# A Fourier mixing layer and a routed feed-forward layer: the third batch's stage 2 in another order beside blocks 1 to 3

## The chip, the cores and the metric

The kernel runs on one core of one Trainium2 chip. Its time is in microseconds (us) of device time for one launch. A core has TensorE (PE in the profile) with its weight loads (PEld), VectorE (DVE), ScalarE (ACT), GpSimd (POOL) and SyncE (SP), which here only issues DMAs. SP and ACT each have a DMA queue of their own; GpSimd issues the indirect DMAs.

## The reference: what is computed

The first half mixes along the sequence, for 8 batches of 2496 positions and 256 channels; the second sends every one of the 19968 tokens through one of 8 experts, chosen by a hash of its id:

```python
X = np.fft.rfft(x, axis=1)
Y = X * (filt_r + 1j * filt_i)[None, :, :]
y = np.fft.irfft(Y, n=x.shape[1], axis=1)
...
expert_idx = token_ids * np.int64(2654435761) % np.int64(E)
for e in range(E):
    xe = x[expert_idx == e]
    out[expert_idx == e] = np.maximum(xe @ w1[e], 0.0) @ w2[e]
```

Everything is float32. w1 is 8 x 256 x 1024, w2 is 8 x 1024 x 256.

## The kernel before, in words

**The Fourier half** splits 2496 into 39 x 64 and takes each batch through three stages, each cut into pieces.

- *Stage 1* (`stage1`, 6 pieces): `load1` brings x (three loads of three DMAs each, L252, on SP's queue); TensorE multiplies by the small table `wf_t` (tiles `pa`, L264 and L270); ACT copies the result to `mid` (L267, L272); a DMA writes it to a scratch tensor d1 in DRAM (L300 on ACT's queue).
- *Stage 2* (`forward` and `back`, 10 pieces each): `load2` brings d1 back in another layout (5 loads, L306, on SP's queue). `forward(u)` multiplies two slices by the table `d_t` (tile `pb_u`, L315). VectorE then multiplies by the filter: L321 makes y from pb and the filter, the two L325 make z, and L326 adds z to y. `back(u)`, the "way back", multiplies y by the table `e_t` (tile `pc_u`, L338); ACT copies it out (L341), and after every second piece ACT issues two DMAs that write it to the scratch tensor d2 (L345).
- *Stage 3* (`stage3`, 6 pieces): `load4` reads d2 (L409, SP's queue, three loads); TensorE multiplies by `wi_t` (tiles `pd`, L264 and L270); ACT copies to `o`; GpSimd scatters the rows to their place among the experts' tokens (L436).

The tiles pa, pb, pc and pd share four PSUM buffers (`fps`); y and z share three SBUF buffers (`ppool`), which are handed out again in the order of the program.

**The expert half** works in tiles of 256 tokens of one expert. A *block* is one such tile, `step(i)`. In the blocks before the 43rd it goes: GpSimd makes four sums of w1 for the tile after (`weight_sums`, tiles `tw`, L881); TensorE makes the up product (`up`, L891, 7 half-size products, after Strassen), while ACT (L895, L902) and VectorE (L898) put its parts together; then SP is given the load of w1 for the tile after next (L467), VectorE transposes the next tile's tokens (L859) and makes its four token sums (tile `st`, L872); then TensorE makes the down product (`down`, tile `dps`, L926) in four quarters of four matmuls; VectorE copies it out (`osb`, L931), and SP is given the load of w2 (L470). GpSimd writes a block's rows to the output (L1019) one block later. The w1 and w2 loads are skipped when the tile two before had the same expert. `load` (L848, ACT's queue, five DMAs) brings the tokens of a later tile.

**The order of the work** around the change is written by hand. Each engine's instructions stand in the order in which the program issues them. All pieces of the Fourier half that go beside the blocks stand in a list `todo` as (due time, piece). A due time of 2.86 means block 2, share .86. `step(i)` calls `run_until` at four points: in front of the down product (due before i + .6), after its first three quarters (before i + .7, .8 and .9), and behind the w2 load (before i + 1). All pieces that are due are issued there. `spaced` makes evenly spaced due times, and `within` moves them into the second half of their block, so that few stand between the up product's parts. `part1`, `part2` and `part3` make such lists for the three stages; `part2` gives the way back of piece u the due time of the forward piece plus a lag.

The first blocks go like this. Before block 0 the program has done batches 0 and 1, stage 1 of batch 2 ("third") and four pieces of stage 1 of batch 3 ("fourth"). Beside blocks 1 to 3 stand stage 2 of the third batch and the last two pieces of the fourth's stage 1; beside blocks 4 to 7 the third's stage 3; from block 6 the fourth's stage 2. Tiles of the second group of blocks may be loaded only when the third batch's rows are scattered.

A DMA of SP or ACT also waits until the DMA that used the same one of eight semaphores before it, counted over both queues in the order of the program, has landed.

## Time and profile before

| what | value |
|---|---|
| median of 6 runs | 1412.92 us (1409.94 to 1416.84) |
| profiled execution, its own time | 1411.95 us |
| its span | 1410.2 us, 26945 instructions |
| busy: PE, PEld, DVE, ACT, POOL | 97%, 90%, 64%, 30%, 59% |
| DMA | 284.67 MB, mean 202 GB/s |
| mean granted TensorE clock | 0.995 of full speed |

How to read it. The profile is of one execution; its span runs from the first to the last instruction, and the time has 1.75 us more around it. A *timeline* line gives the start from the span's start, the time to the end of the merged group, engine, line of the kernel, operation, tile written <- tiles read, shapes, and the number of merged records; in brackets the idle time of that engine ahead of it and what ended it. Each float32 matmul leaves two records, so "x8" is four matmuls, and their modelled ends overlap the next one's start: the distance of two starts is the better measure. A *waits* line reads: engine, tile and line that waited, <- who ended it, total us, times, longest. "<- issue" means that the profile shows no releaser. A *windows* line gives for each stretch its length, the busy time of PE, PEld, DVE, ACT and POOL with the number of instructions, the granted clock (1.00 is full speed), the DMA engines' share, and GB/s.

Blocks in the time of the span: block 0's up product starts at 140.03 us, block 1's at 156.45, block 2's at 181.67, block 3's at 204.17, block 4's at 224.44 and block 5's at 242.02.

### The profile page before, as it was taken

Reading aid. Unit: us, or ns where it says so; the run is one execution under the profiler, and the core shown is the slowest. Engines: PE = TensorE matmul, PEld = TensorE weight load, DVE = VectorE, ACT = ScalarE, POOL = GpSimd, SP = SyncE. Lnnn points to the kernel's source line nnn. Section 1 sums busy time; section 2 is a strip of 40 time slices with the busy share of each in tenths; the row PEclk is TensorE's granted clock in tenths of the full one; section 3 lists DMA queues with packets and bytes.
Section 4 is the critical chain, followed back from the end, with each engine's and each line's share of the span. In section 5 each row is a group of like instructions: output and inputs, shape, how many; then the busy total and the mean of one; then the engine's idle time right before and its main releaser. Section 6 shows DMA issues by size and latency. Waiting matters only on the chain.

```text
span 1410.2 us, 26945 instructions
## 1 busy us (share of the span) xinstructions
PE 1366.0 (97%) x9618; PEld 1273.1 (90%) x9618; DVE 905.6 (64%) x1708; ACT 421.0 (30%) x776; POOL 832.2 (59%) x736
## 2 busy tenths in 40 slices
PE   8898899999999999999999999999999999999997
PEld 7777888989888988899999988899999999999997
DVE  7773675575556566446665687467767677676775
ACT  4554122223232223232223222223222222222222
POOL 6167243844665565578664678787655556655563
PEclk9999899999999999999999999999999999999999
DMA  8777854857987698798896785867643525161611
GB/s 217 216 237 220 239 192 122 274 188 243 264 279 226 186 303 271 252 298 282 285 275 211 220 248 160 234 214 259 198 132 88 174 73 191 45 222 40 215 47 35
DMA packets 253949, 284.67 MB, mean 202 GB/s; under 512 B 125651, under 2 KB 222342, under 8 KB 243620
## 3 DMA queue, kind: packets, MB, share of 16 engines
q1 hardware_dynamic: 104589, 185.62, 41.2%
q10 hardware_dynamic: 129303, 52.69, 15.5%
q0 software_dynamic: 19920, 44.59, 9.1%
q8 instruction: 79, 1.29, 0.4%
q14 instruction: 58, 0.48, 0.1%
HBM read 302.04 MB, written 86.15 MB: 275 GB/s over the span
## 4 chain that ended last, share of the span: by engine, by line
PE 80%; DMA 9%; DVE 5%; issue 3%; POOL 1%; ACT 1%; ACTq 1%; SPq 0%; POOLq 0%; DVEq 0%
PE dps L926 16%; PE up_b L891 7%; PE dnc L953 5%; PE dnb L953 5%; PE dna L953 5%; PE upa L948 5%; PE upc L948 5%; PE up_a L891 4%; PE up_c L891 4%; PE pd L270 4%; PE pb L315 4%; PE pa L270 3%; PE pc L338 3%; PE upe L948 2%; PE upg L948 2%
## 5 line engine op out<-in xcount | busy, mean ns | idle before, releaser
L926 PE MATMUL dps<-wts,ht 128*128 128x256 f32 x1344 | 310.8, 380 | 1.2 <-ACT ht L895 1.2
L1019 POOL DMA_INDIRECT out_dram<-osb,no x158 | 167.9, 1063 | 224.2 <-DVE osb L960 164.3
L926 PEld LDWEIGHTS dps<-wts,ht 128*128 128x128 f32 x1344 | 253.6, 190 | 38.6 <-issue 1.6
L436 POOL DMA_INDIRECT xs<-o,sidx x176 | 176.6, 1003 | 172.5 <-ACT o L272 65.3
L881 POOL TENSOR_TENSOR tw<-wts 128x512 f32<-128x512 f32 x158 | 204.8, 1296 | 88.6 <-DMA wts<-in_moe_w_dram 42.2
L881 POOL TENSOR_TENSOR tw<-wts,tw 128x512 f32<-128x512 f32 x158 | 205.7, 1302 | 6.2
L898 DVE TENSOR_TENSOR ht<-up_b,ht 128x512 f32<-128x512 f32 x126 | 87.1, 691 | 99.1 <-PE up_b L891 75.9
L325 DVE TENSOR_TENSOR z<-pb,filt 64x512 f32<-64x512 f32 x160 | 110.1, 688 | 31.0 <-PE pc L338 29.0
L895 ACT ACTIVATE ht<-ht 128x512 f32<-128x512 f32 x126 | 79.3, 630 | 154.5 <-DVE ht L898 141.1
L957 ACT ACTIVATE ht<-ht 128x512 f32<-128x512 f32 x114 | 71.9, 631 | 155.9 <-DVE ht L960 107.6
L931 DVE COPY osb<-dps 128x512 f32<-128x512 f32 x42 | 29.1, 692 | 121.8 <-PE dps L926 121.4
L891 PE MATMUL up_a<-xt,wts 128*128 128x128 f32 x672 | 97.4, 278 | 5.1 <-DVE xt L859 3.8
L891 PEld LDWEIGHTS up_a<-xt,wts 128*128 128x128 f32 x672 | 89.3, 194 | 8.0 <-issue 4.0
L891 PE MATMUL up_b<-st,tw 128*128 128x128 f32 x672 | 90.6, 278 | 2.9 <-DVE ht L898 1.8
L891 PEld LDWEIGHTS up_b<-st,tw 128*128 128x128 f32 x672 | 82.5, 193 | 5.0 <-issue 4.7
L341 ACT COPY mid<-pc 128x512 f32<-128x512 f32 x60 | 35.0, 583 | 155.9 <-PE pc L338 86.4
L270 PE MATMUL pd<-t,wi_t 120*117 120x256 f32 x320 | 76.5, 380 | 4.4 <-DMA t<-d 2.7
L953 PE MATMUL dna<-wts,ht 128*128 128x128 f32 x608 | 80.3, 275 | 0.0
L898 DVE TENSOR_TENSOR ht<-up_c,ht 128x512 f32<-128x512 f32 x84 | 58.0, 690 | 31.9 <-PE up_c L891 28.2
L948 PE MATMUL upa<-filt,wts 128*128 128x128 f32 x592 | 78.2, 275 | 0.0
L272 ACT COPY o<-pd 117x512 f32<-117x512 f32 x80 | 45.2, 586 | 100.9 <-PE pd L270 42.2
L199 DVE TENSOR_TENSOR filt<-ht 128x512 f32<-128x512 f32 x76 | 57.4, 755 | 26.4 <-ACT ht L957 26.4
(209 smaller groups left out, 2646.5 us busy)
## 6 DMA issues: line engine op xcount, KB each, us to landing
wts<-in_moe_w_dram SPq DMA_DIRECT2D x162, 1024.0 KB
xg<-xs ACTq DMA_DIRECT2D x321, 64.0 KB
d_t<-t2s SPq DMA_DIRECT2D x19, 1024.0 KB
e_t<-t2s SPq DMA_DIRECT2D x19, 1024.0 KB
mid<-d SPq DMA_DIRECT2D x70, 256.0 KB
d<-mid ACTq DMA_DIRECT2D x60, 256.0 KB
x<-in_x_dram SPq DMA_DIRECT2D x39, 312.0 KB
t<-d SPq DMA_DIRECT2D x12, 960.0 KB
```

What stands on the lines that cost most here:

```text
L270: nc.tensor.matmul(out=ps[0:cols * H, k, :], lhsT=w[:], rhs=src[:, 2 * i + k, :], start=True, stop=True)
L325: nc.vector.tensor_tensor(out=z[b], in0=ps[a], in1=f_t[1][64 * hi:64 * hi + 64, s1:s1 + 2, :], op=OP.mult)
L436: st = nc.gpsimd.indirect_dma_start(out=xs[:], out_offset=bass.IndirectOffsetOnAxis(ap=index, axis=0), in_=rows, in_offset=None, bounds_ch ...
L881: eng.tensor_tensor(t[k][:], p, q, op=OP.subtract)
L891: nc.tensor.matmul(out=ps[bank][:, f, :], lhsT=w[:, f * P:(f + 1) * P], rhs=xx, start=first and f == 0, stop=True, skip_group_check=True)
L895: nc.scalar.activation(out=out, in_=in_, func=AF.Relu)
L898: nc.vector.tensor_tensor(out, ps[bank][:], other, op=OP.add)
L926: nc.tensor.matmul(out=ps[:, h, :], lhsT=ht[:, h, fp, :], rhs=w2[:, fp, :], start=(fp == 0), stop=(fp == FP - 1))
L948: nc.tensor.matmul(out=ps[:, f, :], lhsT=w[:, f * P:(f + 1) * P], rhs=xx, start=first and f == 0, stop=True, skip_group_check=True)
L953: nc.tensor.matmul(out=ps[:, 0, :], lhsT=a[:, f, :], rhs=b[:, f, :], start=first and f == 0, stop=True, skip_group_check=True)
L957: nc.scalar.activation(out=out, in_=in_, func=AF.Relu)
L1019: st = nc.gpsimd.indirect_dma_start(out=out[:], out_offset=bass.IndirectOffsetOnAxis(ap=to_rows[i][:, h:h + 1], axis=0), in_=o[:, h, :], i ...
```

## The change

Three lines of the list are replaced by four. The lists of piece times of stage 2 of the third batch are now written out one by one, without `within`.

```diff
-    todo += part2(2, spaced(1, 3.5, N_2), [None] * 4 + [1.5], .6)
-    todo += part3(2, spaced(4.6, 7.5, NU), [4.0, 4.1, 4.8]) + part1(3, [None] * 4 + [1.5, 2], [None, None, .5])
+    todo += [(t, lambda u=u: third.forward(u)) for u, t in enumerate((1.55, 1.65, 1.76, 1.86, 2.56, 2.65, 2.76, 2.86, 3.56, 3.65))]
+    todo += [(t, lambda u=u: third.back(u)) for u, t in enumerate((1.75, 1.85, 1.95, 2.55, 2.75, 2.85, 2.95, 3.55, 3.75, 3.85))]
+    todo += [(1.77, lambda: third.load2(4))]
+    todo += part3(2, spaced(4.6, 7.5, NU), [3.95, 4.1, 4.8]) + part1(3, [None] * 4 + [3.9, 4.2], [None, None, 1.9])
     todo += part2(3, spaced(6.4, 10, N_2), [5.2, 5.4, 5.6, 6.5, 7.5], .6)
```

No instruction is added or removed. In words, in the order in which TensorE takes them:

| | before | after |
|---|---|---|
| block 1, behind up | pb 0, pb 1, dps, pb 2, dps, pb 3, pa 4, dps, pc 0, dps, pc 1 | pb 0, dps, pb 1, dps, pc 0, pb 2, dps, pc 1, pb 3, dps, pc 2 |
| block 2, behind up | pb 4, pa 5, pc 2, pb 5, dps, pb 6, pc 3, dps, pb 7, pc 4, dps, dps, pc 5 | pc 3, pb 4, dps, pb 5, dps, pc 4, pb 6, dps, pc 5, pb 7, dps, pc 6 |
| block 3, behind up | pb 8, pc 6, pb 9, dps, pc 7, dps, pc 8, dps, dps, pc 9 | pc 7, pb 8, dps, pb 9, dps, pc 8, dps, pc 9, dps, pa 4 |
| block 4, behind up | dps, dps, dps, pd 0, dps | dps, pa 5, dps, dps, pd 0, dps |

(dps is a quarter of the down product; pa 4 and pd 0 are pairs of two tiles; pa is the fourth batch's, all else the third's.) VectorE and ACT follow in the same order. On SP's queue the third x load of the fourth batch moves from between the loads of w1 and w2 of tile 2 to behind w2 of tile 3; the first t load (L409, of d2) moves from behind w1 of tile 6 to in front of it, behind w2 of tile 5; the second stays behind w1 of tile 6. ACT's two DMAs that write the fourth batch's last stage 1 pieces to d1 (L300) move from block 2 to block 4.

## The prediction

> **What bounds the kernel now.** I read the page first (busy shares, chain), then PE's waits between the end of block 1's up product (162.70 us of the span) and the end of block 4 (242.02), then the PE, VectorE and GpSimd timelines of that stretch.

> ```profile
> PE 1366.0 (97%) x9618; PEld 1273.1 (90%) x9618; DVE 905.6 (64%) x1708; ACT 421.0 (30%) x776; POOL 832.2 (59%) x736
> PE 80%; DMA 9%; DVE 5%; issue 3%; POOL 1%; ACT 1%; ACTq 1%; SPq 0%; POOLq 0%; DVEq 0%
> ```

> TensorE is busy 97% of the span and is most of the chain that ended last: nothing in this change removes a matmul, so all it can win is PE's idle time, and all it can lose is new idle time. PE's waits from 157 to 242 us:

> ```profile
> PE pa L270 <- issue: 3.3, 1, 3.3
> PE pd L270 <- DMA t<-d: 1.6, 1, 1.6
> PE up_b L891 <- DVE ht L898: 1.4, 2, 0.9
> PE pc L338 <- DVE y L326: 1.0, 1, 1.0
> ```

> The largest stands in block 1 (PE timeline):

> ```profile
> 167.02 1.89 PE L926 MATMUL dps<-wts,ht 128*128 128x256 f32 x8
> 168.74 1.03 PE L315 MATMUL pb<-mid,d_t 128*128 128x256 f32 x4
> 173.07 3.59 PE L270 MATMUL pa<-x,wf_t 117*120 117x256 f32 x8 [3.30 <-issue]
> 176.49 1.89 PE L926 MATMUL dps<-wts,ht 128*128 128x256 f32 x8
> ```

> The pa pair is the fourth batch's stage 1 piece 4. It needs x, whose three loads SP issues from 163.27 to 169.76. Then it runs 3.42 us where a pair takes 1.73, because of the clock:

> ```profile
> 135.40:138.82 3.42, 0.79 (x8) 0.60 (x6) 0.00 (x0) 0.00 (x0) 2.64 (x3) 1.00 0.52 93
> 138.82:145.65 6.83, 5.62 (x26) 5.65 (x27) 3.60 (x7) 0.59 (x1) 2.34 (x2) 0.50 0.85 194
> 169.54:172.96 3.42, 0.23 (x2) 0.00 (x0) 3.31 (x6) 0.00 (x0) 1.22 (x2) 1.00 0.60 202
> 172.96:176.37 3.41, 3.30 (x8) 2.61 (x9) 2.02 (x3) 0.59 (x1) 0.00 (x0) 0.50 0.84 311
> ```

> After a 3.4 us stretch with PE busy 0.23 or 0.79 us, the granted clock is 0.50 in the next one or two.

> **What PE loses now.** Start-to-start on the timeline: pb or pc 0.865 us, pa or pd pair 1.73, the short pa 1.08, a quarter of dps 1.73, a whole up product 6.25 (156.45 to 162.70). From 162.70 to 242.02 PE does 10 pb and 10 pc (17.3), pa 1.73 + 1.08, pd 1.73, 16 quarters of dps (27.7), 3 up (18.75): 68.3. The stretch is 79.3, so **11.0 us are lost**: block 1 5.1 (3.4 wait, 1.7 half clock); up of block 2 1.25 and of block 3 0.73 (L898 late, VectorE backlog); block 3 1.2 (pc waits for y); up of block 4 0.83 (ACT late after pc's copies); block 4 1.86 (pd waits for t).

> **The change, part by part.** The same instructions are issued, in another order; only waits move.

> *Stage 1 pieces 4 and 5 and their x load go later.* The 3.4 us wait for x and its 1.7 us go: the load is issued behind block 3's w2 load, the piece stands at the end of block 3, some 25 us later. On SP the next weight loads move up: tile 3's w1 is issued at about 167 instead of 172.15. Piece 5's ACT writes of d1 move to block 4; the fourth batch reads d1 in block 5 at the earliest, more than 10 us behind. I take nothing for these two; the cover is that slack.

> *The new order in block 1.* PE's order becomes pb_0, dps, pb_1, dps, pc_0, pb_2, dps, pc_1, pb_3, dps, pc_2. From 162.70, pc_0 is due at 162.70 + 0.87 + 1.73 + 0.87 + 1.73 = 167.9. It needs y_0, and y_0 is VectorE's (timeline of VectorE, then of GpSimd):

> ```profile
> 164.24 0.60 DVE L872 TENSOR_TENSOR st<-xt 128x128 f32<-128x128 f32 x1
> 164.88 1.31 DVE L872 TENSOR_TENSOR st<-st,xt 128x128 f32<-128x128 f32 x1
> 166.11 1.35 DVE L872 TENSOR_TENSOR st<-xt 128x128 f32<-128x128 f32 x1
> 167.38 1.35 DVE L872 TENSOR_TENSOR st<-xt,st 128x128 f32<-128x128 f32 x1
> 168.66 0.68 DVE L321 TENSOR_TENSOR y<-pb,filt 128x512 f32<-128x512 f32 x1
> 169.35 1.39 DVE L325 TENSOR_TENSOR z<-pb,filt 64x512 f32<-64x512 f32 x2
> 170.78 0.69 DVE L326 TENSOR_TENSOR y<-y,z 128x512 f32<-128x512 f32 x1
> ```
> ```profile
> 163.41 1.28 POOL L881 TENSOR_TENSOR tw<-wts 128x512 f32<-128x512 f32 x1 [22.25 <-PE up_b L891]
> ...
> 167.27 1.32 POOL L881 TENSOR_TENSOR tw<-wts,tw 128x512 f32<-128x512 f32 x1
> ```

> The token sums L872 take 1.3 us each beside GpSimd's tw, and 0.29 us in block 2 where it is idle. Nothing before this point is moved, so y_0 ends at 171.47 again. Now pb_2, pb_3 and pa stand between; in the changed order pc_0 stands there at once, and **PE waits from 167.9 to 171.55, 3.65 us**. What is late next is y_0, not x. Behind pc_0 in PE's queue stand all of block 1's rest and the next up.

> *Half clock after that wait.* The trace does not show this wait: the price lies between 0 (the gap of 2.07 us before 47.59 left the clock at 1.0) and 3.4 (half of the 6.83 us at 138.82). The halved stretches keep a beat of their own (138.82 and 172.96 lie 34.14 = 10 x 3.414 us apart), so one of them will hold between 1.8 and 3.4 us of the 3.65; nearest is the stretch at 169.54, so 1.7, which I give 6 in 10.

> [...]

> *Rest of block 1 and up of block 2.* y_1 ends by about 175.3 (its last add is beside tile 3's tw, which now starts near 172; such adds took 0.95 to 1.74 against 0.69); pc_1 is due 175.0 at full clock, after 176 at half: 0 to 0.4. VectorE no longer holds z for pc (now "z L325 <- PE pc L338", 4.2 us at 179.28), so the osb copy and L898 are in time: the 1.25 and 0.73 go, for about 0.

> *Block 2.* Counted from the up's end, y_4 is ready at +6.35 (before: 189.17 and 195.52, with an add of 1.74 beside tw); pc_4 is due at +6.07; pc_5 about the same. 0 to 0.9, I take 0.5.

> *Block 3.* First y at +7.9 from the up's end, since tw is again beside the sums (before: 211.15 and 219.04). pc_8 is due after pc_7, pb_8, dps, pb_9, dps: 6.06. It waits 1.9, then pc_9 0.3: 2.2 instead of 1.2.

> *Block 4.* pc_9 ends 1.0 to 3.5 us sooner against block 4's up, ACT's copy is free: the 0.83 goes. The t load is issued when d2 has landed, at the latest 5.9 us after its issue on ACT (225.25 to 231.17 today): 1.4 to 4 us into block 4's up. It took 7.3 us to pd (231.17 to 238.47). pd is due at 6.25 + 1.73 + 1.08 + 3.46 = 12.5. The 1.86 goes. SP stands still till d2 has landed; behind it is the next w1 load, not due before +5.6.

> **Sum.** New losses: 3.65 + 1.7 + 0 + 0.5 + 2.2 = 8.05, and 0.3 for restarts behind waits (first matmul 0.45 to 0.47 instead of 0.38): **8.35 against 11.0, a gain of 2.7**; without the half clock (and 0.2 at pc_1) 6.85, a gain of 4.2. The profiled execution took 1411.95 (span 1410.2): 1409.25 or 1407.8. It lies 0.97 under the median of the six runs, 1412.92, from which the same gains give 1410.2 and 1408.7. Both versions roll the same dice with the clock, so I put the forecast between: **1409.6**. Behind 242 us PE runs without idle time to 320, so the gain reaches the end.

> [...]

> **Rivals.**
> 1. *y_0 is on time.* If the token sums ran at 0.29 us as in block 2, y_0 would end 6.35 - 1.05 = 5.3 us after the up, due is 5.19: the 3.65 + 1.7 go too, gain 8.0: 1404.9. For it: block 2 does just that. Against: tw of tile 2 waits for nothing that the change moves. Chance 0.18, 1403 to 1407.
> 2. *The change moves waits and wins nothing.* The half clock holds two stretches (+1.7, as at 138.82), block 2 costs 0.9: 10.5 against 11.0, 1412.4. Chance 0.14, 1411.6 to 1414. That the t load does not come sooner belongs here: if it still missed pd by 1.86, gain 0.8.
> 3. *Slower: the t load.* pd_0 has 12.5 us, the load is issued at 1.4 to 4 and took 7.3. If d2's writes and this load together take over 3.9 us more than that, pd waits; over 6.6 more and the kernel is slower than before. At twice 7.3 for the load and 4 for the issue, pd waits 6.1: 2.7 - 6.1, 1416.3. Against: fewer loads are beside it than now. Chance 0.08, 1414 to 1418.

> The forecast's own case has 0.60, 1407.5 to 1411.6. A measurement tells 0.3%, 4.24 us, from no change. Faster than 1408.7: rival 1 (0.18) and half of the forecast without the half clock, which lies on that bound (0.12): 0.30. Slower than 1417.2: the worse part of rival 3 and what I do not see, 0.08. Same: 0.62. The range leaves out the far end of rival 1 and rival 3: 1405 to 1413.5.

> **What would show it.** PE idle about 3.6 us in front of the first pc (L338), released by VectorE's y L326, in place of pa <- issue; granted clock 0.50 for 3.4 us behind it, or not; no wait of up_b for L898 in blocks 2 and 3; about 1.9 us in front of pc_8; no pd <- t; the end of block 4 at 238 to 239.5 instead of 242.02. If pc_0 doesn't wait, rival 1 holds and I misread VectorE's queue; if pd waits, rival 3.

## The result and the profile after

The changed kernel takes 1408.87 us, median of 26 runs (1403.76 to 1412.57), beside 1413.6 for the kernel before (52 runs). The medians differ by 4.7 us. The ratio is 0.9963, with a 95% interval of 0.9952 to 0.9974: 5.2 us faster, 3.7 to 6.8. The prediction was 1409.6, a gain of 3.3 over the 1412.92 of the first six runs. The profiled execution has a span of 1405.8 us (before: 1410.2). Its page, the busy shares:

```profile
PE 1367.3 (97%) x9618; PEld 1274.4 (91%) x9618; DVE 911.8 (65%) x1708; ACT 419.8 (30%) x776; POOL 833.7 (59%) x736
```

Busy shares say nothing here: PE is at 97% in both. PE's waits from 157 to 242 us do. The four lines that the prediction shows, and a fifth of 0.2 us, have become one:

```profile
PE pc L338 <- DVE y L326: 5.7, 2, 3.9
```

pa no longer waits, nor pd, nor up_b for VectorE. The PE timeline shows where the two waits stand (the first pc of block 1, pc_0, and pc_8 of block 3) and that pa and pd have no bracket:

```profile
172.25 1.13 PE L338 MATMUL pc<-y,e_t 128*128 128x256 f32 x4 [3.88 <-DVE y L326]
...
216.14 1.10 PE L338 MATMUL pc<-y,e_t 128*128 128x256 f32 x4 [1.80 <-DVE y L326]
...
221.66 1.89 PE L270 MATMUL pa<-x,wf_t 117*120 117x256 f32 x8
...
236.01 1.89 PE L270 MATMUL pd<-t,wi_t 120*117 120x256 f32 x8
```

The half clock came too. In the windows (length, busy time of PE, PEld, DVE, ACT and POOL, granted clock, DMA share, GB/s) PE is busy 1.03 of 3.41 us, and the next stretch has 0.50:

```profile
169.87:173.28 3.41, 1.03 (x5) 0.93 (x6) 3.30 (x6) 0.00 (x0) 1.61 (x2) 1.00 0.93 315
173.28:176.69 3.41, 3.41 (x10) 2.70 (x9) 3.32 (x5) 0.59 (x1) 2.62 (x2) 0.50 0.46 180
```

y_0 is late for the reason that the prediction gives. VectorE's token sums (L872 before, L874 now) last 1.00 to 1.35 us beside GpSimd's tw, and y_0 ends at 172.19, 9.17 us behind the up product; SP gave out the w1 load that tw needs at 163.86 in this execution. VectorE, then GpSimd, then SP:

```profile
164.57 1.00 DVE L874 TENSOR_TENSOR st<-xt 128x128 f32<-128x128 f32 x1
165.60 1.32 DVE L874 TENSOR_TENSOR st<-st,xt 128x128 f32<-128x128 f32 x1
...
171.50 0.69 DVE L326 TENSOR_TENSOR y<-y,z 128x512 f32<-128x512 f32 x1
```
```profile
164.15 1.27 POOL L883 TENSOR_TENSOR tw<-wts 128x512 f32<-128x512 f32 x1 [22.59 <-PE pb L315]
```
```profile
163.86 0.11 SPq L467 DMA_DIRECT2D wts<-in_moe_w_dram  x1
```

tw starts 0.19 us behind the end of that issue, while tile 3's tw starts 5.5 us behind the issue of its load (168.53 to 173.99). So tile 2's load seems to be one of those that are skipped, and tw waits for SP to come to it and not for its bytes.

All profiles side by side, from the starts of the up products on PE's timeline. The columns 1 to 2, 2 to 4 and 4 to 5 are the distances between the up products of blocks 1 to 2, 2 to 4 and 4 to 5; without waits they would be 19.23, 39.32 and 16.0 in the new order, 74.55 in all (68.3 of the prediction and the up product of block 1).

| profile | 1 to 2 | 2 to 4 | 4 to 5 | 1 to 5 | half clock from | 10 to 25 |
|---|---|---|---|---|---|---|
| before | 25.22 | 42.76 | 17.59 | 85.58 | 172.96 | 286.59 |
| before_again | 24.72 | 43.41 | 17.70 | 85.83 | 172.35 | 286.04 |
| before_3 | 23.41 | 42.81 | 17.63 | 83.85 | none | 286.31 |
| after | 25.04 | 41.58 | 16.08 | 82.70 | 173.28 | 284.70 |
| after_2 | 24.46 | 41.60 | 16.08 | 82.13 | 175.38 | 283.37 |
| after_3 | 23.35 | 41.60 | 16.08 | 81.03 | 172.99 | 286.80 |
| e1_stage1_later | 19.46 | 46.78 | 17.40 | 83.65 | 184.79 | 285.57 |
| e2_order_alone | 23.94 | 41.03 | 16.94 | 81.92 | none | 284.69 |
| e3_w1_sooner | 19.48 | 41.59 | 16.08 | 77.14 | none | 284.86 |
| e4_dummy | 22.33 | 41.60 | 16.08 | 80.00 | none | 285.89 |
| e5_fill_block3 | 19.48 | 39.86 | 16.08 | 75.42 | none | 285.21 |
| e6_old_order_w1 | 18.34 | 43.05 | 18.15 | 79.53 | none | 285.48 |
| e7_best | 19.48 | 39.87 | 16.08 | 75.42 | none | 286.44 |

### The profile page after: what moved, and what is told of

Same layout as the page of the kernel before. It is cut to its first block, busy times and chain, and to the rows that moved or that the text cites. A ratio compares the mean times of both kernels' runs of the same rounds, so it can differ in the third digit from the quotient of the medians.

```text
span 1405.8 us, 26942 instructions
## 1 busy us (share of the span) xinstructions
PE 1367.3 (97%) x9618; PEld 1274.4 (91%) x9618; DVE 911.8 (65%) x1708; ACT 419.8 (30%) x776; POOL 833.7 (59%) x736
## 4 chain that ended last, share of the span: by engine, by line
PE 77%; DMA 12%; DVE 5%; issue 2%; POOL 1%; ACTq 1%; ACT 1%; SPq 0%; POOLq 0%; DVEq 0%
PE dps L928 16%; PE up_b L893 6%; PE dnc L955 5%; PE dna L955 5%; PE dnb L955 5%; PE upa L950 4%; PE upc L950 4%; PE up_a L893 4%; PE up_c L893 4%; PE pd L270 4%; PE pb L315 4%; PE pa L270 3%; PE pc L338 3%; DMA xg<-xs 2%; PE upe L950 2%
## 5 line engine op out<-in xcount | busy, mean ns | idle before, releaser
L325 DVE TENSOR_TENSOR z<-pb,filt 64x512 f32<-64x512 f32 x160 | 110.1, 688 | 24.1 <-PE pc L338 22.0
L897 ACT ACTIVATE ht<-ht 128x512 f32<-128x512 f32 x126 | 79.3, 630 | 154.5 <-DVE ht L900 138.6
L893 PEld LDWEIGHTS up_b<-st,tw 128*128 128x128 f32 x672 | 82.2, 193 | 3.5 <-issue 2.8
L270 PE MATMUL pd<-t,wi_t 120*117 120x256 f32 x320 | 76.4, 380 | 2.3 <-DVE z L325 1.7
L315 PE MATMUL pb<-mid,d_t 128*128 128x256 f32 x280 | 74.2, 389 | 0.4 <-DVE z L325 0.4
```

Source lines behind the costliest of these rows:

```text
L270: nc.tensor.matmul(out=ps[0:cols * H, k, :], lhsT=w[:], rhs=src[:, 2 * i + k, :], start=True, stop=True)
L315: nc.tensor.matmul(out=ps[:, i, :], lhsT=d_t[:, s, :], rhs=rhs, start=True, stop=True)
L325: nc.vector.tensor_tensor(out=z[b], in0=ps[a], in1=f_t[1][64 * hi:64 * hi + 64, s1:s1 + 2, :], op=OP.mult)
L893: nc.tensor.matmul(out=ps[bank][:, f, :], lhsT=w[:, f * P:(f + 1) * P], rhs=xx, start=first and f == 0, stop=True, skip_group_check=True)
L897: nc.scalar.activation(out=out, in_=in_, func=AF.Relu)
```

## The experiments

The theory: the change exchanges pa's wait for x against pc_0's wait for y_0; what it gains lies in the later stage 1 pieces, VectorE's backlog and the t load; and y_0 is late because tw meets the token sums. The rival: the new order itself is the gain. Ratios are against the kernel before on the same chip, with 95% intervals.

**The later pieces alone.** The kernel before, with

```diff
-part1(3, [None] * 4 + [1.5, 2], [None, None, .5])
+part1(3, [None] * 4 + [3.9, 4.2], [None, None, 1.9])
```

> One part of the change alone: the kernel before, with the fourth batch's last two stage 1 pieces and its third x load put later, and nothing else. My theory: two things gain in the change, that pa no longer waits for x (3.4 us of wait and 1.7 us of half clock in block 1), and that up of blocks 2 and 3 and pd are no longer held up (about 2 and 1.9 us); the wait of pc_0 for y_0 eats the first of them. Here the ways back stay where they were, so pc_0 stands behind pb_2, pb_3 and three quarters of the down product and meets y_0 about in time: block 1 loses at most 0.5 us instead of 5.1, and the kernel is 4 to 5 us faster than before, about as fast as the whole change. L898 in front of up_b still holds up block 2 (about 1 us), pd still waits for t (about 1.9 us or more). Rival, the new order is what gains and the later pieces only make room: then this one alone gains at most 1.5 us, because the end of block 4 comes at 240.5 us or later.

Measured: 1407.89 us, ratio 0.9946 (0.9924 to 0.9968), 4.5 to 10.7 us faster: as fast as the whole change within the intervals, and the rival's 1.5 at most is out. PE's waits of its profile, the slowest of its ten executions:

```profile
PE up_b L891 <- DVE ht L898: 3.0, 2, 2.6
PE pc L338 <- DVE y L326: 1.8, 2, 1.0
PE pd L270 <- DMA t<-d: 1.1, 1, 1.1
```

In detail I was off twice. Block 1 loses 1.1 us and not 0.5: y_1's add met tw of tile 3, whose load now came earlier, and took 1.55 us. And VectorE's backlog at block 2 was 2.6 us, with a half clock behind it, not 1: a wait that goes lets PE arrive sooner at the next one. The profiled stretch, 83.65 us, is only 1.4 us under the mean of the three profiles of before (85.1), so the gain of the timed runs is not accounted for by this profile.

**The new order alone.** The changed kernel, with those pieces, the x load and the t load due as before:

```diff
-part3(2, spaced(4.6, 7.5, NU), [3.95, 4.1, 4.8]) + part1(3, [None] * 4 + [3.9, 4.2], [None, None, 1.9])
+part3(2, spaced(4.6, 7.5, NU), [4.0, 4.1, 4.8]) + part1(3, [None] * 4 + [1.5, 2], [None, None, .5])
```

> The other part alone: the new order of stage 2's pieces, with the fourth batch's stage 1 pieces, its x load and the third batch's t load due when they were before. My theory: pc_0 stands in front of pb_2 and waits 3.6 to 3.9 us for y_0 as in the whole change, with the half clock behind it (1.7 us on a mean); the x load is early again, but piece 4 now stands behind pc_0 and finds x there, so it waits less than 1 us; L898 no longer holds up blocks 2 and 3; pd waits for t by 0 to 2 us. In all 0.5 to 2.5 us faster than before. Rival, the order gains by itself: 4 us or more faster than before. Second rival, x and y_0 add up: pa waits again by 2 us or more, and the kernel is as slow as before or slower.

Measured: 1412.67 us, ratio 0.9998 (0.9976 to 1.002): between 3.4 faster and 2.8 slower. PE's waits:

```profile
PE pc L338 <- DVE y L326: 4.4, 2, 2.6
PE pd L270 <- DMA t<-d: 1.8, 1, 1.8
```

A gain of 4 by the order is out. In the profile pa stands behind pc_0 and finds its x there, so x and y_0 do not add up there, as the second rival had it; its other half, as slow as before, is what the timed runs show. The profile, at 81.92 us from block 1 to 5, flatters: it is the fastest of its twelve executions and drew no half clock in this stretch. By time alone, the gain of the change is that of the later pieces; how the two parts share it within the stretch, one profile of each doesn't tell.

**tw out of the way of the sums.** The changed kernel, with loads and writes that stood ahead of the w1 load of tile 2 on SP's queue issued behind block 0's up product:

```diff
-head += [(125 + .1 * g, lambda g=g: third.load2(g)) for g in range(4)]
+head += [(125 + .1 * g, lambda g=g: third.load2(g)) for g in range(2)]
-head += [(126, lambda: [nc.sync.dma_start(out=dram, in_=chip) for dram, chip in put_off[3]])]
+todo += [(t, lambda g=g: third.load2(g)) for g, t in ((2, .3), (3, .31))]
+todo += [(.32, lambda: [nc.sync.dma_start(out=dram, in_=chip) for dram, chip in put_off[3]])]
```

> The changed kernel, with the w1 load of tile 2 some places earlier on SP's queue: two of the third batch's stage 2 loads and six writes, which stood in front of it, are issued behind block 0's up product instead. GpSimd can then make tw of tile 2 while PE does block 1's up, and is idle when VectorE makes the token sums. My theory: the sums take about 0.3 instead of 1.3 us, y_0 ends about 5.3 us behind the up product instead of 9.2, pc_0 waits less than 1 us instead of 3.9 and no half clock follows: 3.5 to 5.5 us faster than the changed kernel. Rival: y_0 is late for something else (pb, or VectorE's own queue), the sums stay over 1 us or pc_0 waits 3 us or more all the same, and the time is within 1 us of the changed kernel. If the loads of stage 2 that come later hold up pb_2 or pb_3 instead, that shows as a pb wait for d and takes some of the gain back.

Measured: 1404.9 us, ratio 0.9920 (0.9893 to 0.9948). VectorE, GpSimd and SP in its profile (the sums are L875 here, tw L884), and PE's waits:

```profile
164.27 0.29 DVE L875 TENSOR_TENSOR st<-xt 128x128 f32<-128x128 f32 x1
164.60 0.29 DVE L875 TENSOR_TENSOR st<-st,xt 128x128 f32<-128x128 f32 x1
...
167.33 0.69 DVE L326 TENSOR_TENSOR y<-y,z 128x512 f32<-128x512 f32 x1
```
```profile
154.18 1.27 POOL L884 TENSOR_TENSOR tw<-wts 128x512 f32<-128x512 f32 x1 [13.18 <-DMA xg<-xs]
```
```profile
153.88 0.11 SPq L467 DMA_DIRECT2D wts<-in_moe_w_dram  x1
```
```profile
PE pc L338 <- DVE y L326: 1.8, 1, 1.8
```

tw is done at 159.2, the sums take 0.29 us, y_0 ends at 168.02, 5.29 us behind the up product (162.73), pc_0 starts 0.17 us late, no half clock follows, and block 1 is 5.56 us shorter than in the changed kernel's first profile (3.9 to 5.6 than in its three). The 1.8 us left are pc_8's. This is the cause of the long wait, shown. In time it is 4.0 us by the medians, inside the 3.5 to 5.5 expected; the two ratios' intervals just miss each other.

**Dummies in the wait.** The changed kernel and `todo += [(1.749, lambda: warm(14))]`, in front of pc_0.

> The changed kernel with 14 matmuls of 128x128 (about 3.1 us, on constants; their result is used by nothing) just in front of pc_0, where PE waits 3.9 us for y_0. It adds work that the reference does not ask for. My theory: the wait is what halves the clock behind it; with PE busy in it the granted clock stays 1.00 from 165 to 180 us, pc_0 still starts at about 172.2 us since y_0 is not touched, and the kernel is 1 to 1.7 us faster than the changed one. Rival: the halving at 173.28 us has another cause (what PE did a few us earlier, or none in this stretch): then the clock is 0.50 there all the same and the time is unchanged; and if the dummies come to stand behind y_0, up to 0.5 us slower.

Measured: 1406.66 us, ratio 0.9945 (0.9921 to 0.9969). The windows over the dummies and behind them:

```profile
166.20:169.62 3.42, 3.42 (x25) 3.21 (x24) 3.36 (x7) 0.00 (x0) 2.64 (x3) 1.00 0.62 97
...
173.03:176.44 3.41, 3.41 (x18) 3.00 (x17) 3.32 (x5) 0.59 (x1) 3.15 (x3) 1.00 0.26 103
```

No half clock with PE busy, as the theory has it. But y_0 ended 7.36 us behind the up product here, so the wait without dummies would have been about 2.2 us, and the new order alone kept its clock with a wait of 2.58: that the dummies saved the clock is in agreement with this profile, not shown by it. Nor can the price be read from it: pc_0 started at 171.00 right behind the dummies, and the interval overlaps that of the change.

**Filling block 3's wait.** The kernel with w1 sooner, and piece 4 of the fourth's stage 1 at 3.745 instead of 3.9, in front of pc_8:

```diff
-part1(3, [None] * 4 + [3.9, 4.2], [None, None, 1.9])
+part1(3, [None] * 5 + [4.2], [None, None, 1.9]) + [(3.745, lambda: fourth.stage1(4))]
```

> The kernel with the w1 load of tile 2 sooner, and the fourth batch's stage 1 piece 4 one place earlier in block 3: in front of pc_8, where PE waited 1.8 us for y_8, instead of behind pc_9. My theory: that wait is VectorE's alone, pa needs nothing of VectorE and its x landed long ago, so the pair (1.73 us) fills the wait and PE waits at most 0.2 us there: 1.5 to 1.9 us faster than with w1 sooner alone. Rival: pa's ACT copies or its PSUM buffer come in pc_8's way, and the wait only moves to pc_8 or pc_9: within 0.5 us.

Measured: 1402.79 us, ratio 0.9925 (0.9902 to 0.9948), the lowest median of all: 7.4 to 13.9 us faster than before. PE's timeline:

```profile
212.64 1.89 PE L270 MATMUL pa<-x,wf_t 117*120 117x256 f32 x8
214.62 1.10 PE L338 MATMUL pc<-y,e_t 128*128 128x256 f32 x4
```

pa takes the place of the wait, and the way from block 2 to block 4 is 1.73 us shorter in the profile. No timed difference from w1 sooner alone is shown: the medians differ by 2.1 us, but they were taken on different chips, and against before on the same chip the ratios are 0.9925 here and 0.9920 there.

**The old order with tw out of the way.** The first experiment and the SP lines of the third together.

> The fourth cell of the square: the old order of stage 2's pieces, with the fourth batch's stage 1 pieces later (as in the first experiment) and the w1 load of tile 2 sooner (as in the third). It asks what the new order is worth once x and tw are out of the way. My theory: pc_0 and pc_1 wait for nothing (0.9 us less than in the first experiment), but VectorE, whose z waits for the ways back that stand two to four pieces behind, still holds up the up products of blocks 2 and 3 through L898 (1 to 3 us), pc_8 waits about 1 and pd about 1.1: 1.5 to 3.5 us slower than the changed kernel with w1 sooner. Rival: VectorE's backlog came from the token sums, not from the order; then L898 is in time and it is within 1 us of that kernel or faster.

Measured: 1405.38 us, ratio 0.9947 (0.9929 to 0.9966). PE's waits:

```profile
PE pd L270 <- DMA t<-d: 1.8, 1, 1.8
PE up_b L892 <- DVE ht L899: 1.1, 2, 0.6
PE pc L338 <- DVE y L326: 1.0, 1, 1.0
```

From block 1 to 5 it takes 79.53 us beside 77.14 in the new order: 2.4 more, inside the 1.5 to 3.5 expected. The timed medians, of different chips, differ by 0.5 us, and the ratios, 0.9947 and 0.9920, have intervals that overlap, so this is the profile's verdict only. Nor is it faster than the first experiment by ratio (0.9946). Of the backlog at block 2, 2.6 us in the first experiment, 0.6 is left: most of it went with the sums, as the rival said; that the rest comes from the order, and pd from the t load, is argued from the waits that the new order doesn't have.

**Dummies before block 0.** The kernel of block 3's filled wait with `warm(30)` instead of `warm(14)` ahead of block 0.

> The kernel with w1 sooner and piece 4 in front of pc_8, and 30 instead of 14 dummy matmuls before block 0 (16 more of 128x128, some 3.6 us, whose result nothing uses): it fills the wait of 3.3 to 4.2 us in which PE stands for the first tokens, behind which the clock was halved for 6.83 us in almost all profiles. My theory: the wait in front of a stretch is what halves it, so the clock is 1.00 from 135 to 150 us and the kernel is 1.5 to 3.4 us faster than without the dummies, with a mean granted clock higher by 0.001 to 0.0025. Rival: the halving there has another cause and stays: no difference.

Measured: 1406.58 us, ratio 0.9957 (0.9939 to 0.9976): no gain, and my theory falls. The half clock at 139 us is gone, but PE's waits from 140 to 156 us have a new line, and the windows show a half clock behind that:

```profile
PE dps L929 <- ACT ht L898: 3.7, 1, 3.7
```
```profile
148.18:151.59 3.41, 0.12 (x2) 0.00 (x0) 2.30 (x6) 0.73 (x2) 0.00 (x0) 1.00 0.43 105
151.60:155.01 3.41, 2.98 (x7) 2.45 (x8) 0.00 (x0) 1.41 (x3) 0.00 (x0) 0.50 0.85 247
```

ACT must make ht (L898) for block 0's down product, and stands behind its own token loads (xg) until a DMA of xg ends the wait (`ACT ht L898 <- DMA xg<-xs: 8.0, 1, 8.0`). With w1 sooner and with block 3 filled, where the clock was halved for 6.83 and 3.41 us here, the down product starts 9.57 and 9.55 us behind the start of the up product, with PE waiting 0.3 and 1.5 us for ACT's ht: ACT set that time, and the half clock filled time that PE would have waited anyway. Here it starts at 10.92; why ACT was later still is open. (The expectation's 6.83 us does not hold for all: the half clock at this place lasted 6.83 us in the first profile of before and with w1 sooner, 3.41 in the changed kernel's first and with block 3 filled.)

**Before and after again.** Unchanged copies, for a second and a third profile.

> The kernel before once more, for a second profile. In the profiled pair the changed kernel won 1.9 us between the up products of blocks 10 and 25, where both issue the same instructions: before took 286.59 us for that way, the changed kernel 284.71, and the experiments so far 285.57 (old order, stage 1 later), 284.69, 284.86 and 285.90. If before loses there because of its order (DMAs that run later), it takes 286.3 us or more again. If that was the luck of one execution, it takes 284.6 to 286.

> The kernel before, a third profile, to stand beside those of the changed kernel. Its first two profiles took 85.57 and 85.82 us from the start of block 1's up product to the end of block 4. If x's load is as steady as it seems, 84.5 to 86.5 us again; from block 10 to block 25 (286.59 and 286.05 us so far) 285 to 286.6, as all experiments.

> The changed kernel once more, for a second profile: the measured gain is about 5 us, my sum gives 2.7, and the profiled pair gives 2.9 between the start of block 1's up product and the end of block 4. Theory A, the profiled execution was a bad draw at y_0: how far the token sums meet tw depends on when SP gets its DMA semaphores (y_0 ended 9.2 us behind the up product there, but 7.2 to 7.4 us in two experiments with the same order), and the half clock does not always follow. Then pc_0 starts 1 to 2 us sooner here, 13.5 to 14.6 us behind the start of block 1's up product instead of 15.5, and the way to the end of block 4 takes 79 to 82 us instead of 82.7. Theory B, the stretch is as in the profiled execution (82.2 us or more) and the rest of the gain lies elsewhere or in the clock.

> The same, a third profile of the changed kernel. Theory A: the start of block 1's up product to the end of block 4 in 79 to 82 us. Theory B: 82.2 us or more again.

Measured: see the table. before_again took 286.04 from block 10 to 25, in neither expected range; before_3 gave 83.85 us from block 1 to 5, under the expected 84.5, and no half clock fell in it. The changed kernel took 82.13 and 81.03 from block 1 to 5, pc_0 starting 14.89 and 13.79 us behind the start of block 1's up product (15.47 in the first profile). after_3 is theory A; after_2 lies between the two theories and misses A's range for pc_0 by 0.3 us. In after_3 two of the four sums escaped tw. (The two experiments that the expectation takes its 7.2 to 7.4 us from show 7.36 and 7.87.)

One line of before has to be read with care. In its first profile pa waited for "issue"; in the third the waits say

```profile
PE pa L270 <- DVE y L326: 3.1, 1, 3.1
```

The timelines of SP and PE in that third profile:

```profile
167.47 8.41 SPq L252 DMA_DIRECT2D x<-in_x_dram  x3
179.34 1.96 PE L270 MATMUL pa<-x,wf_t 117*120 117x256 f32 x8 [3.11 <-DVE y L326]
```

pa doesn't read y. In the three profiles it starts 3.3, 3.4 and 3.5 us behind the end of the third x issue on SP (169.76, 167.59 and 175.88), whatever y does, and in the new order alone, behind pc_0, it waits for nothing. The wait was x's, as the prediction had it.

## Why the prediction was right, and where it was off

- *pc_0 waits for y_0, 3.65 us.* Right in cause (third experiment). Measured 3.88, 3.30 and 2.20. The step "so y_0 ends at 171.47 again" was too firm: the end differs by execution, 7.5 to 9.2 us behind the up product with the change, by how far tw, which waits for SP, meets the sums.
- *Half clock behind it, 1.7 us at 6 in 10.* It came in all three profiles of the changed kernel, behind windows of 3.41 us with PE busy 1.03, 0.24 and 1.30, and in none with the wait gone or filled. The new order alone waited 2.58 us there, with 1.87 in the window, and had none.
- *pc_1 and the up products of blocks 2 and 3 wait for nothing.* Right: their lines are gone, and the start of block 2 to that of block 3 takes 20.07 us, with no wait in it.
- *Block 2, 0.5 us.* Wrong, 0: tile 4's tw started at 196.70, too late to meet y_4.
- *Block 3, 2.2 us.* 2.3 in all three profiles (21.52 against 19.23).
- *Block 4, the t load.* Right: pd waits for nothing (16.08 us against 17.6). The load was issued 0.5 us into block 4's up product, sooner than the 1.4 to 4 of the prediction, and rival 3 did not come. Its margin of "over 3.9 us" held only for the early end of that range; for a load issued at 4 it was 12.5 - 4 - 7.3 = 1.2.
- *The sum.* Losses of 8.35 or 6.85 predicted; 8.2, 7.6 and 6.5 measured (1 to 5 less 74.55). For before I used 11.0; three profiles give 11.0, 11.3 and 9.3. On the means, 10.5 - 7.4 = 3.1 us are gained here, as predicted (2.7 to 4.2).
- *"PE runs without idle time to 320, so the gain reaches the end."* It does, but not it alone: the mean from block 10 to 25 is 286.3 before and 285.0 after, 1.4 us more, though both issue the same there. The changed kernel's three values span 3.4 us, so whether the change moves DMAs there or this is chance stays open. PE's wait for ACT (up_a behind ht) is 1.1 to 2.1 us on that way before and 0.3 to 2.7 in the changed kernel, so it varies in both. This step did not hold as written: I looked for no difference behind block 4, and the gain, forecast at 3.3, is 5.2. That the forecast time lies only 0.7 us off is in part luck: the six runs it starts from have a median 0.7 us under that of all 52.
- *Rival 1, y_0 on time at +5.3, 1404.9 us.* It didn't happen, but the third experiment builds it: +5.29 and 1404.9.

Why the token sums are slow beside tw no run shows; how slow they are, the profiles do: 0.28 to 0.29 us each with tw done at 159.2 (third experiment), 1.00 to 1.35 with tw running from 164.15 (the changed kernel's first).

## What to carry to other kernels

Before moving a piece out of a wait, ask when the next piece in that place has its input: here x's wait was exchanged for y_0's, and about as much as the change won (4.0 us beside its 4.7, by the medians) lay two engines away, in when SP gives out the load that GpSimd works on while VectorE is needed. Where the timing of two engines sets a wait, read it from several profiles, since one execution is one draw. And before repairing a half clock, ask what else is late behind it: the one at 139 us went with the dummies ahead of block 0, and with ACT late behind it nothing was gained (ratio 0.9957 beside 0.9925).

## What the runs showed of the hardware

```profile
139.15:142.56 3.41, 1.56 (x12) 1.43 (x13) 2.56 (x5) 0.59 (x1) 2.40 (x2) 1.00 0.76 155
142.56:145.97 3.41, 3.41 (x19) 3.41 (x18) 1.14 (x2) 0.00 (x0) 0.00 (x0) 0.50 0.92 225
```
```profile
210.59:214.00 3.41, 1.59 (x8) 1.11 (x7) 3.30 (x6) 0.00 (x0) 0.00 (x0) 1.00 0.26 45
214.00:217.41 3.41, 3.38 (x17) 2.67 (x16) 1.78 (x3) 0.88 (x2) 0.00 (x0) 1.00 0.02 5
```

The edge is not sharp. Another window with 1.87 us of work, and this one was followed by 0.50, from the profile of block 3's filled wait:

```profile
10.98:14.39 3.41, 1.87 (x18) 1.81 (x17) 1.59 (x10) 1.12 (x2) 0.00 (x0) 1.00 0.89 231
14.39:17.81 3.42, 3.42 (x18) 3.42 (x18) 3.11 (x18) 0.88 (x2) 2.18 (x5) 0.50 0.92 212
```

So in these rows 1.95 us or more of idle time in one window (3.41 - 1.46) was always followed by a half clock, 1.54 to 1.85 sometimes, and where a wait fell on the beat decided: 2.20 us in the changed kernel's third profile left 1.30 of work in its window and halved the clock, 3.11 us (pa in the third of before) left 1.56 and did not. An estimate from these rows, with the edge put at 1.85 and PE busy otherwise: a wait W between 1.85 and 3.7 us halves it at (W - 0.29) / 3.41 of all positions. For 3.65 us that is nearly always, not the 6 in 10 that I had put, and for 2.2 us a little over half.

The first 140 us, which the change does not touch, also differ by execution: block 0's up product starts between 138.72 and 146.49 us in the thirteen profiles. Among the profiles of one kernel that is the largest difference seen: 7.8 us in the three of before and 3.6 in those of the changed kernel, beside 2.0 and 1.7 in the stretch.
